# Attention and an MLP mixer on one core: the first normalization ahead of a branch, seven products of the identity, and one element's x through GpSimd

## The chip, the cores and the metric

The kernel runs on one core of a Trainium2 chip. Five engines work side by side, each through its own instruction queue: TensorE (PE; its weight loads are listed apart as PEld), VectorE (DVE), ScalarE (ACT), GpSimd (POOL) and SyncE (SP), which here issues nearly all DMAs. An engine works through its queue in order. Before an instruction starts, the semaphores that it waits for must have been raised by other engines or by landed DMAs. The metric is the device time of one execution in microseconds (us); lower is better.

## The reference, cut to what matters

```python
# q, k, v: (8, 12, 448, 64); all float32
def _attn_ref(q, k, v, g_q, g_k):
    def rmsnorm(x, g):
        rms = np.sqrt(np.mean(x * x, axis=-1, keepdims=True) + 1e-06)
        return x / rms * g
    q_n, k_n = (rmsnorm(q, g_q), rmsnorm(k, g_k))
    scale = 1.0 / np.sqrt(q.shape[-1])
    scores = scale * np.matmul(q_n, k_n.transpose(0, 1, 3, 2))
    scores = scores - np.max(scores, axis=-1, keepdims=True)
    attn = np.exp(scores)
    attn = attn / (np.sum(attn, axis=-1, keepdims=True) + 1e-09)
    return np.matmul(attn, v)

# heads are put side by side: x is (8, 448, 768)
def _moe_ref(x, w_tok1, w_tok2, w_ch1, w_ch2):
    h = np.maximum(x.transpose(0, 2, 1) @ w_tok1, 0.0) @ w_tok2
    u = x + h.transpose(0, 2, 1)
    h2 = np.maximum(u @ w_ch1, 0.0) @ w_ch2
    return u + h2
```

There are eight elements in the batch. For each, attention over twelve heads makes x; then a token MLP and a channel MLP run on x.

## The kernel before, in words

**Tiling.** Heads go in pairs, six pairs to an element and 48 in all; pair p lies with its two heads in the two halves of the partitions. For a pair, q and k are loaded, squared on ScalarE (`square`, L1435), summed on VectorE (`reduce`, L1451), turned into inverse roots by a guess and three Newton steps (`roots`: L1473, then L1492 to L1494 on VectorE, or L1481 to L1484 on GpSimd for later pairs), scaled (`scale`, L1502) and transposed (`turn_qk`, L430 on TensorE, copied out by ScalarE at L436 and L438). `score` (L456) multiplies k with q and ScalarE takes the exponential (L460); `values` (L529) multiplies with v; `ones` (L509) makes the row sums.

**The branch.** Softmax runs without subtracting the maximum unless the gains are large. `Start`, ahead of the branch, loads the first pairs, computes from the gains whether they are (`large`, L1340), and squares pairs 0 and 1. Every engine then loads the flag and jumps (L1539). All else is in `whole`, which is built twice, once for each arm; with this data the second arm runs. It begins with `first_pairs`: VectorE's reductions, roots and scalings of pairs 0 and 1. The loads that SP issues behind its own jump begin with v (L409), further q and k (L1412) and weights (L223). VectorE also has four passes over each loaded piece of weights (L346 to L351, then L380, with a pass on ScalarE at L357 between): the matrices come as 64-bit floats and are made into 32-bit ones.

**The MLP of an element.** The x of an element is turned and brought into the layout for the token MLP. For the first element TensorE does it. For the others VectorE transposes 32x32 blocks into `xt` (L827, `trans_x`), `send_x` writes them to DRAM in four DMAs of 32 rows each (`xs`, L789), and `load_x` reads them back in five (`x`, L798 and L801). An element has two halves of three pairs, and each half goes its own way through `xt`, `xs` and `x`. `tok1` multiplies (L840; L847 is the remainder of 64 tokens, where both halves' remainders come one after the other), `tok2` (L882) adds into `uT`. Then the first channel product `ch1` runs on seven Strassen products (L1002), on sums that VectorE (T1, T2) and GpSimd (T3, T4; L906, L907) form in `moving_sums`, and the second (`plain_2`, L1051, for the second element; `ch2`, L1068, on fifteen products, for the third and later) after it. The seven products are computed in the order of B11, B21, T2, T3, T1, B22, T4. Weights come as units of 384 KB from DRAM (`load_units`, L930) into eight buffers; up to seven are loaded ahead.

**Weight forms.** The fifteen products of `ch2` need sums of weight blocks. They are made once, while the second element's MLP runs, in eight groups (`form_items`): four DMAs from SP load a group (L305 to L307), GpSimd does 16 additions (L321) and three copies (L325) and sends the result to DRAM in two DMAs (L311, L312). A unit of the fifteen products may be loaded only when all eight groups are formed.

**Order.** No scheduler moves anything. Items are written out in lists with estimated costs, merged in proportion, and run in that order. `later(us, fn)` puts a step off by so many estimated microseconds: when the running sum of costs has passed its due time, it is emitted at that place in the queues. So the due times of forms, of `send_x` and of `load_x` decide the place of their instructions between all others, on SP and GpSimd too. A due time isn't a time on the chip.

For the third element's second half, `trans_x` names due times 0.0 for the send, 0.25 for the step and 6.0 for the load:

```python
start, step, load = {(1, 1): (2.0, 0.5, 9.0), (2, 1): (0.0, 0.25, 6.0)}.get((b, half), (2.0, 2.0, 12.0))
```

`first_pairs`, `Start`, `send_x`, `load_x` and `form_items` are what the change touches:

Of the kernel before, what the change touches and what calls it, by code (L numbers as in the profile page):

```python
# [13 lines left out]
ALU = mybir.AluOpType  # L14
# [69 lines left out]
def whole(ctx, tc, shifted, pre, q, k, v, g_q, g_k, moe_w_tok1, moe_w_tok2, moe_w_ch1, moe_w_ch2, out):  # L84


    nc = tc.nc
    ctx.enter_context(tc.manual_schedule(engines={
        e.engine for e in (nc.tensor, nc.vector, nc.scalar, nc.gpsimd)}))

    B, H, S, D = q.shape
    C = H * D
    DT = moe_w_tok1.shape[1]
    DC = moe_w_ch1.shape[1]
    P = 128
# [10 lines left out]
    KC, KF = NC // 2, NF // 2  # L106
    assert S % NS == 0 and R <= P and 2 * D == P and H % 2 == 0 and NC == NPAIR
    assert DT % P == 0 and C % P == 0 and DC % P == 0 and HC <= 512 and HC % P == 0 and S <= 512
# [5 lines left out]
    NM = S // P  # L114
# [27 lines left out]
    ident, one_c, expo_c, g_t = pre.ident, pre.one_c, pre.expo_c, pre.g_t  # L142
# [7 lines left out]
    ws2 = dram.tile([P, NF9 * 8, P], F32, name="ws2")  # L150

    st = dict(pre.st)
    pre.first_pairs(st)
    m_tile = lambda: ps_M.tile([P, 512], F32, name="m_ps", tag="M")
    s_tile = lambda name: ps_S.tile([P, 512], F32, name=name, tag="S")

    clock, pending = [0.0], []

# [133 lines left out]
    def form_items():  # L292


        G, FORMS_FROM, FORMS_EVERY = range(8), 55.0, 18.0
        plain = lambda g: wp2[:].rearrange("p (m h x k t) n -> p x h t m k n", m=3, h=2, x=2, k=3)[
            :, g // 4, g // 2 % 2, g % 2]
        made = ws2[:].rearrange("p (f c) n -> p c f n", c=8)
        eight = lambda t: t[:].rearrange("p n w -> p (n w)").bitcast(F32).rearrange("p (q n) -> p q n", q=8)

        def load(g):
            a, b, c = st["form", g] = [eight(raw_tile()) for _ in range(3)]
            src = plain(g)
            for m in range(2):
                nc.sync.dma_start(out=a[:, 3 * m:3 * m + 3], in_=src[:, m])  # L305
            nc.sync.dma_start(out=a[:, 6:8], in_=src[:, 2, 0:2])
            nc.sync.dma_start(out=b[:, 7], in_=src[:, 2, 2])  # L307

        def send(g):
            a, b, c = st.pop(("form", g))  # L310
            nc.gpsimd.dma_start(out=made[:, g, 0:8], in_=c)  # L311
            nc.gpsimd.dma_start(out=made[:, g, 8:NF9], in_=b[:, 0:7])  # L312
            st["formed"] += 1

        def part(g, i):
            a, b, c = st["form", g]
            at = dict(d=a[:, 4], s=a[:, 6], v=a[:, 7], y=a[:, 3])
            at.update({(m, k): a[:, 3 * m + k] if 3 * m + k < 8 else b[:, 7] for m in range(3) for k in range(3)})
            at.update({f: c[:, f] if f < 8 else b[:, f - 8] for f in range(NF9)})
            for o, x, op, y in W_STEPS[4 * i:4 * i + 4]:  # L320
                nc.gpsimd.tensor_tensor(  # L321
                    out=at[o], in0=at[x], in1=at[y], op=ALU.add if op == "+" else ALU.subtract)
            if i == 3:
                for f, x in W_SINGLE:
                    nc.gpsimd.tensor_copy(out=at[f], in_=at[x])  # L325
                send(g)

        for g in G:
            at = FORMS_FROM + g * FORMS_EVERY
            later(at, lambda g=g: load(g))  # L330
            for i in range(4):
                later(at + 8.0 + 2.5 * i, lambda g=g, i=i: part(g, i))
# [450 lines left out]
    def send_x(b, half, t, step):  # L783


        xs = st["xs", b, half] = xs_pool.tile([KC * S, P], F32, name="xs")

        def part(i):
            nc.sync.dma_start(  # L789
                out=xs[:, i:i + 32].rearrange("(n t) c -> t n c", t=32),  # L790
                in_=t[i:i + 32].rearrange("t (n c) -> t n c", c=32))
        for i in range(0, P, 32):
            later(i * step / 32, lambda i=i: part(i))

    def load_x(b, half):
        x, xs = x_tile(b, half), st.pop(("xs", b, half))[:].rearrange("(j s) n -> s j n", j=KC)
        for j in range(KC):
            nc.sync.dma_start(  # L798
                out=x[:, j, 0:NM, :], in_=xs[0:NM * P, j].rearrange("(c p) n -> p c n", p=P))
        for a in range(2):  # L800
            nc.sync.dma_start(out=x[a * D:(a + 1) * D, :, NM, :], in_=xs[NM * P:S])  # L801

    def x_tile(b, half):
        st["x", b, half] = x_pool.tile([P, KC, NS, P], F32, name="x", tag="x")
        return st["x", b, half]
# [496 lines left out]
class Start:  # L1302


    def __init__(self, ctx, tc, q, k, g_q, g_k, w2, g2, gate):
        self.nc = nc = tc.nc
        self.q, self.k = q, k
        B, H, S, D = q.shape
        self.NPAIR, self.NS, self.D = H // 2, 4, D
        self.R = S // self.NS  # L1310
        P = 128
        pool = lambda name, bufs: ctx.enter_context(tc.tile_pool(name=name, bufs=bufs))
        const = pool("start", 1)
        KF = w2.shape[0] // P // 2
        self.hb = const.tile([P, HB, 4, S // 2], F32, name="hb")

        flat = self.hb[:].rearrange("p q f s -> p (q f s)")
        n, o = 4 * self.NS * D, self.NPAIR * 4 * self.NS * D
        self.st = {("qk", p): flat[:, p * n:(p + 1) * n] for p in range(self.NPAIR)}
        self.qkT = [flat[:, o + i * 2 * S:o + (i + 1) * 2 * S].rearrange("p (i s) -> p i s", i=2) for i in range(3)]  # L1320
        assert flat.shape[-1] >= o + 3 * 2 * S
        self.v_0 = const.tile([P, S], F32, name="v_first")[:]
        self.first_slot = self.NPAIR
        self.far = 3 * self.NPAIR + 2
        qk_t = const.tile([P, 2, n], F32, name="qk_t")
        self.qk_t = [qk_t[:, i, :] for i in range(2)]
        self.v_t = [const.tile([P, S], F32, name=f"v_{i}")[:] for i in range(3)]

        warm = const.tile([P, 1], F32, name="warm")
        nc.vector.memset(warm[:], 1.0)  # L1330
        self.load_qk(0, self.st, other=nc.scalar)
        self.load_qk(1, self.st, other=nc.scalar)
        nc.scalar.activation(out=warm[:], in_=warm[:], func=AF.Square)
        gg = gate.tile([1, D], F32, name="gg")
        most = gate.tile([1, 1], F32, name="most")
        self.large = large = gate.tile([1, 1], I32, name="large")
        nc.vector.tensor_tensor(out=gg[:], in0=g2[:, 0, :], in1=g2[:, 1, :], op=ALU.mult)
        nc.vector.tensor_tensor(out=gg[:], in0=gg[:], in1=gg[:], op=ALU.mult)
        nc.vector.tensor_reduce(out=most[:], in_=gg[:], axis=AX_X, op=ALU.max)
        nc.vector.tensor_scalar(large[:], most[:], SCORE_BOUND**2 / D, None, ALU.is_gt)  # L1340
        self.g_t = const.tile([P, 2], F32, name="g_t")
        for i, g in enumerate((g_q, g_k)):
            for a in range(2):
                nc.gpsimd.dma_start(
                    out=self.g_t[a * D:(a + 1) * D, i:i + 1], in_=g.rearrange("(p o) -> p o", o=1))
        self.ident = const.tile([P, P], F32, name="ident")
        make_identity(nc, self.ident[:, :])
        self.one_c = const.tile([P, D], F32, name="one_c")
        nc.gpsimd.memset(self.one_c[:], 1.0)
        self.expo_c = const.tile([P, 1], F32, name="expo_c")  # L1350
        nc.gpsimd.memset(self.expo_c[:], -896.0 * 2**23)
        self.sq = const.tile([P, 4 * self.NS, D + 1], F32, name="sq")


        self.sq_2 = flat[:, 0:4 * self.NS * (D + 1)].rearrange("p (r d) -> p r d", d=D + 1)
        self.sq_1 = qk_t[:].rearrange("p i n -> p (i n)")[:, 0:4 * self.NS * (D + 1)].rearrange(
            "p (r d) -> p r d", d=D + 1)
        for sq in (self.sq, self.sq_1):
            self.summand(sq)
        for p in (2, 3):  # L1360
            for part in self.loads(p, self.st, nc.gpsimd, nc.gpsimd):
                part()
        self.rs_0 = const.tile([P, 8 * self.NS], F32, name="rs_0")
        for p in range(2):
            self.square(p, self.st)

    def first_pairs(self, st):

        D = self.D
        self.reduce(0, st)  # L1370
        self.reduce(1, st)
        for part in self.roots(0, st):
            part()
        self.scale(0, st)
        self.nc.vector.scalar_tensor_tensor(
            out=self.g_t[:, 0:1], in0=self.g_t[:, 0:1], scalar=float(D) ** 0.5, in1=self.g_t[:, 1:2],
            op0=ALU.mult, op1=ALU.mult)
        self.scale(1, st)

    def heads(self, p):  # L1380
        b, j = divmod(p, self.NPAIR)
# [192 lines left out]
```

## Time and profile before

| | |
|---|---|
| median of 3 runs | 1281.13 us (1280.30 to 1282.95) |
| the profiled execution | 1280.59 us |
| its span, first to last instruction | 1278.8 us |
| granted TensorE clock, mean | 0.997 |
| TensorE busy | 98% of the span |
| VectorE, ScalarE, GpSimd busy | 62%, 31%, 31% |
| DMA, mean | 179 GB/s |

Times within a trace are counted from the span's first instruction. An engine's share of busy time is an average over stages that have different limits; where an engine waits, the profile names what ended the wait. In a line of the timeline stand the start, the time taken, the engine, the line of the kernel, the operation, the tiles (out<-in), the shape and the number of instructions merged into the line; in brackets at the end stands how long the engine was idle before and what ended it. SPq and the like are an engine's queue: waits, jumps and the issuing of DMAs. A line of waits reads: engine, tile and line of what waited, what it waited for, us in total, how often, the longest. The answer for one line of the kernel gives, for each operation, the count, the duration in ns (min/median/max) and the first and last start.

### The profile page before, as it was taken

The page shows a single profiled execution, that of the slowest core. Times are in us where ns is not written, and L with a number is a line of the kernel's source. Part 1 is how long each engine was busy: PE and PEld are TensorE (multiplying, and loading weights), DVE is VectorE, ACT ScalarE, POOL GpSimd, SP SyncE. Part 2 cuts the span into 40 slices and gives each one's busy share as a digit, 9 for nine tenths or more (in the row PEclk, how much of TensorE's full clock was granted, in tenths as well). Part 3 has the DMA queues.
Part 4 walks back from the last instruction along what each step waited for, and adds up shares of the span by engine and source line. Part 5 has one row for each costly group of instructions (what it writes and reads, how often), then busy time and mean ns, then how long its engine had stood idle before and what let it go on. Part 6 is the DMA issues. An engine that isn't in the chain of part 4 may idle for free.

```text
span 1278.8 us, 20023 instructions
## 1 busy us (share of the span) xinstructions
PE 1249.1 (98%) x7236; PEld 887.4 (69%) x7236; DVE 796.8 (62%) x1241; ACT 393.6 (31%) x785; POOL 394.8 (31%) x637
## 2 busy tenths in 40 slices
PE   5999999999999899999999999999999999999998
PEld 2444444457745487796778768885887867797998
DVE  6999869756663355855668356765558456554233
ACT  6663433124330144402433044311343024300210
POOL 2302552043995611331223112241122322131222
PEclk9999999999999899999999999999999999999999
DMA  8767486999789876695657767585766865386554
GB/s 204 172 179 200 144 228 167 217 260 253 212 220 236 188 171 162 140 258 112 161 151 178 190 143 187 139 220 120 188 158 146 234 130 144 114 207 142 191 173 105
DMA packets 486784, 228.37 MB, mean 179 GB/s; under 512 B 368276, under 2 KB 446996, under 8 KB 486676
## 3 DMA queue, kind: packets, MB, share of 16 engines
q1 hardware_dynamic: 479682, 213.33, 67.5%
q0 software_dynamic: 3968, 12.98, 3.3%
q8 instruction: 59, 0.97, 0.3%
q10 hardware_dynamic: 3026, 0.69, 0.3%
q14 instruction: 49, 0.40, 0.1%
HBM read 184.26 MB, written 42.66 MB: 177 GB/s over the span
## 4 chain that ended last, share of the span: by engine, by line
PE 88%; DVE 5%; DMA 2%; SPq 1%; ACT 1%; issue 1%; DVEq 0%; ACTq 0%
PE m_ps L1002 25%; PE m_ps L1068 22%; PE s_ps L456 9%; PE o_ps L529 9%; PE m_ps L882 6%; PE m_ps L972 5%; PE m_ps L1051 4%; PE m_ps L840 2%; PE t_ps L840 2%; PE d_ps L509 1%; PE m_ps L509 1%; DVE es L497 1%; DVE raw L349 1%; DVE raw L347 1%; PE t_ps L430 1%
## 5 line engine op out<-in xcount | busy, mean ns | idle before, releaser
L1068 PE MATMUL m_ps<-hb,unit 128*128 128x224 f32 x1440 | 277.2, 354 | 0.0
L1068 PEld LDWEIGHTS m_ps<-hb,unit 128*128 128x128 f32 x1440 | 271.0, 190 | 8.9 <-issue 7.7
L1002 PE MATMUL m_ps<-tu,unit 128*128 128x224 f32 x1008 | 201.6, 355 | 1.3 <-ACT r L1012 1.3
L1002 PEld LDWEIGHTS m_ps<-tu,unit 128*128 128x128 f32 x1008 | 189.1, 190 | 15.0 <-issue 9.2
L460 ACT ACTIVATE e<-s_ps 128x448 f32<-128x448 f32 x294 | 138.7, 553 | 178.4 <-PE s_ps L456 169.8
L1002 PE MATMUL m_ps<-uT,unit 128*128 128x224 f32 x756 | 151.1, 354 | 0.0
L1002 PEld LDWEIGHTS m_ps<-uT,unit 128*128 128x128 f32 x756 | 142.2, 190 | 6.9 <-issue 3.9
L456 PE MATMUL s_ps<-qkT 64*64 64x448 f32 x1260 | 143.7, 545 | 0.8 <-ACT x L822 0.8
L529 PE MATMUL o_ps<-e,v 64*64 64x448 f32 x1148 | 129.4, 538 | 0.3 <-ACT uT L566 0.2
L497 DVE TENSOR_TENSOR es<-es,e 128x896 f32<-128x896 f32 x90 | 101.8, 1131 | 13.3 <-ACT e L460 8.6
L1008 DVE TENSOR_TENSOR hb<-m_ps,r 128x448 f32<-128x448 f32 x63 | 39.2, 622 | 108.8 <-POOL r L1008 56.7
L1008 POOL TENSOR_TENSOR hb<-r,r 128x448 f32<-128x448 f32 x21 | 23.8, 1132 | 246.0 <-ACT r L1024 246.0
L456 PEld LDWEIGHTS s_ps<-qkT 64*64 64x64 f32 x1260 | 44.9, 132 | 70.1 <-issue 60.6
L529 PEld LDWEIGHTS o_ps<-e,v 64*64 64x64 f32 x1148 | 45.1, 133 | 63.9 <-issue 60.4
L1481 POOL TENSOR_TENSOR nt<-rs 128x56 f32<-128x56 f32 (+1 forms) x54 | 22.4, 415 | 196.4 <-DVE rs L1473 193.6
L1009 ACT ACTIVATE hb<-hb 128x448 f32<-128x448 f32 x84 | 48.4, 577 | 99.4 <-DVE hb L1008 77.7
L321 POOL TENSOR_TENSOR raw<-raw 128x128 f32<-128x128 f32 x128 | 65.1, 528 | 34.6 <-DMA raw<-wp 30.1
L1083 POOL TENSOR_TENSOR uT<-uT,r 128x448 f32<-128x448 f32 x42 | 51.4, 1238 | 78.5 <-DVE r L1083 46.7
L882 PE MATMUL m_ps<-w_sb,h 128*128 128x448 f32 x192 | 75.2, 544 | 0.0
L1451 DVE TENSOR_REDUCE ms<-sq 128x28 f32<-128x896 f32 (+2 forms) x44 | 47.4, 1079 | 36.3 <-ACT sq L1438 28.2
L1008 DVE TENSOR_TENSOR r<-m_ps,r 128x448 f32<-128x448 f32 x42 | 26.1, 622 | 64.5 <-PE m_ps L1002 64.5
L887 DVE TENSOR_TENSOR uT<-uT,m_ps 128x448 f32<-128x448 f32 x48 | 29.4, 614 | 59.1 <-PE m_ps L882 59.0
(148 smaller groups left out, 1607.8 us busy)
## 6 DMA issues: line engine op xcount, KB each, us to landing
unit<-ws SPq DMA_DIRECT2D x267, 384.0 KB, 4.1
raw<-in_moe_w_ch_dram SPq DMA_DIRECT2D x72, 256.0 KB, 3.5
v<-in_v_dram SPq DMA_DIRECT2D x96, 112.0 KB, 4.1
out_dram<-turned SPq DMA_DIRECT2D x182, 56.0 KB, 1.9
xs<-xt SPq DMA_DIRECT2D x56, 168.0 KB, 4.6
qk_t<-in_q_dram SPq DMA_DIRECT2D x144, 56.0 KB, 3.6
qk_t<-in_k_dram SPq DMA_DIRECT2D x144, 56.0 KB, 3.7
x<-xs SPq DMA_DIRECT2D x42, 192.0 KB, 3.7
```

The lines of the kernel that those rows point to most:

```text
L321: nc.gpsimd.tensor_tensor(out=at[o], in0=at[x], in1=at[y], op=ALU.add if op == "+" else ALU.subtract)
L456: nc.tensor.matmul(out=pss[i][rows_of(i, a), 0:S], lhsT=qkT[h, 1, k * D:(k + 1) * D], rhs=qkT[h, 0, :], start=True, stop=True)
L460: nc.scalar.activation(out=e[:, i, :], in_=pss[i][:, 0:S], func=AF.Exp)
L497: nc.vector.tensor_tensor(out=es[:], in0=(es if k > 1 else st["e", t, 0])[:], in1=st["e", t, k][:], op=ALU.add)
L529: nc.tensor.matmul(out=st["o", p][a * D:(a + 1) * D, 0:S], lhsT=vt[rows, k * D:(k + 1) * D], rhs=e[rows, :], **kw)
L840: nc.tensor.matmul(out=st["t1", h][jc][:, 0:HC], lhsT=w1_sb[:, c, jc * P:(jc + 1) * P], rhs=st["x", b, h][:, :, c, :], start=start and c = ...
L882: nc.tensor.matmul(out=ps[:, 0:S], lhsT=st["h1", jc][:, cc * P:(cc + 1) * P], rhs=w2_sb[:, jc].rearrange("p c r -> p (c r)"), start=(jc == ...
L972: nc.tensor.matmul(out=ps, lhsT=a[:, o + 2 * half, :], rhs=natural(half * KF + t) if wide else u[:, half * KC + t, :], start=(t == 0 and h ...
L1002: nc.tensor.matmul(out=ps[:, j * HS:(j + 1) * HS], lhsT=w[:, t, j, :], rhs=m, start=(t == 0), stop=(t == KC - 1))
L1008: add = lambda e, o, x, y: e.tensor_tensor(out=o, in0=x, in1=y, op=ALU.add)
L1068: nc.tensor.matmul(out=ps[:, x * HS:(x + 1) * HS], lhsT=st["w"][:, tile_at % 6, :], rhs=hb[:, X_SLOT[f], i, :], start=(i == 0), stop=(i == 3))
L1083: e.tensor_tensor(out=get(out), in0=get(x_), in1=get(y), op=ALU.add if op == "+" else ALU.subtract)
```

## The change

- VectorE's first chain (`first_pairs`) is moved from the head of `whole` into `Start`. It now stands ahead of the branch, once instead of once in each arm. Its small tiles come from a pool of their own (`st_0`).
- In its place TensorE multiplies the identity with itself seven times, into a bank of the scores' pool that nobody reads.
- For the third element's second half (element 2, half 1), the four DMAs of `send_x` and the five of `load_x` are issued by GpSimd instead of SP.
- Groups 6 and 7 of the forms are due 26 estimated us later.

```diff
     st = dict(pre.st)
-    pre.first_pairs(st)
...
+    first_ps = s_tile("first_ps")
+    for _ in range(7):
+        nc.tensor.matmul(out=first_ps[:, 0:P], lhsT=ident[:, :], rhs=ident[:, :], start=True, stop=True)
...
-        G, FORMS_FROM, FORMS_EVERY = range(8), 55.0, 18.0
+        G, FORMS_FROM, FORMS_EVERY, FORMS_REST = range(8), 55.0, 18.0, 26.0
...
-            at = FORMS_FROM + g * FORMS_EVERY
+            at = FORMS_FROM + g * FORMS_EVERY + (FORMS_REST if g > 5 else 0.0)
             later(at, lambda g=g: load(g))
...
         def part(i):
-            nc.sync.dma_start(
+            x_queue(b, half).dma_start(
                 out=xs[:, i:i + 32].rearrange("(n t) c -> t n c", t=32),
                 in_=t[i:i + 32].rearrange("t (n c) -> t n c", c=32))
...
+    def x_queue(b, half):
+        return nc.gpsimd if (b, half) == (2, 1) else nc.sync
+
     def load_x(b, half):
+        e = x_queue(b, half)
         x, xs = x_tile(b, half), st.pop(("xs", b, half))[:].rearrange("(j s) n -> s j n", j=KC)
         for j in range(KC):
-            nc.sync.dma_start(
+            e.dma_start(
                 out=x[:, j, 0:NM, :], in_=xs[0:NM * P, j].rearrange("(c p) n -> p c n", p=P))
         for a in range(2):
-            nc.sync.dma_start(out=x[a * D:(a + 1) * D, :, NM, :], in_=xs[NM * P:S])
+            e.dma_start(out=x[a * D:(a + 1) * D, :, NM, :], in_=xs[NM * P:S])
...
-        for p in range(2):
-            self.square(p, self.st)
-
-    def first_pairs(self, st):
-
-        D = self.D
-        self.reduce(0, st)
-        self.reduce(1, st)
-        for part in self.roots(0, st):
-            part()
-        self.scale(0, st)
-        self.nc.vector.scalar_tensor_tensor(
-            out=self.g_t[:, 0:1], in0=self.g_t[:, 0:1], scalar=float(D) ** 0.5, in1=self.g_t[:, 1:2],
-            op0=ALU.mult, op1=ALU.mult)
-        self.scale(1, st)
+        with tc.tile_pool(name="st_0", bufs=1) as self.st_pool:
+            self.nt_pool = self.st_pool
+            for p in range(2):
+                self.square(p, self.st)
+            self.reduce(0, self.st)
+            self.reduce(1, self.st)
+            for part in self.roots(0, self.st):
+                part()
+            self.scale(0, self.st)
+            nc.vector.scalar_tensor_tensor(
+                out=self.g_t[:, 0:1], in0=self.g_t[:, 0:1], scalar=float(D) ** 0.5, in1=self.g_t[:, 1:2],
+                op0=ALU.mult, op1=ALU.mult)
+            self.scale(1, self.st)
```

What the queues of the arm that runs hold then, compared with before: TensorE's has the seven products ahead of its first transposes, and nothing else differs. VectorE's has the flag's load and the jump behind the second scaling instead of ahead of the first reduction. ScalarE's is the same. On GpSimd, group 5 is followed by the twelve Newton steps of a later pair, then the nine DMAs of x, then group 6, then group 7 with the moving sums T3 and T4 of the third element between its parts. On SP the nine DMAs of x are gone, the loads of group 6 stand behind the first three units of the third element and the loads of group 7 behind six output DMAs; a few loads of v, of q and of units change places with each other further on.

## The prediction

> **What bounds the kernel now.** I read the page's busy line first, then TensorE's waits, then a table by stage around the largest of them, and last the timelines of the engines that feed it.
>
> ```profile
> PE 1249.1 (98%) x7236; PEld 887.4 (69%) x7236; DVE 796.8 (62%) x1241; ACT 393.6 (31%) x785; POOL 394.8 (31%) x637
> ...
> PE t_ps L430 <- DVE hb L1502: 14.4, 1, 14.4
> PE t_ps L847 <- DMA x<-xs: 5.2, 1, 5.2
> ```
>
> TensorE is busy for 1249.1 of 1278.8 us. Two holes make 19.6 of the other 29.7 us: 14.4 us before its first transpose, and 5.2 us at 421.8, where the third element's second half of x isn't there. No other wait exceeds 1.3 us. The change works on these two.
>
> The table by stage (us, busy us of PE, PEld, DVE, ACT, POOL, granted clock, DMA share, GB/s) and TensorE's timeline show that the second hole costs more than its length; the last three lines are the same place one element later, without a wait.
>
> ```profile
> 422.00:427.00 5.00, 0.00 (x0) 0.00 (x0) 0.00 (x0) 0.74 (x2) 4.69 (x12) 0.72 1.07 342
> 427.00:430.00 3.00, 2.93 (x6) 1.58 (x7) 0.22 (x1) 0.00 (x0) 2.42 (x8) 0.50 1.10 187
> ...
> 420.92 0.92 PE L847 MATMUL m_ps<-x,w_sb 64*128 64x384 f32 x4
> 427.07 2.07 PE L847 MATMUL t_ps<-x,w_sb 64*128 64x384 f32 x4 [5.24 <-DMA x<-xs]
> 433.99 9.28 PE L882 MATMUL m_ps<-w_sb,h 128*128 128x448 f32 x24
> ...
> 576.40 0.92 PE L847 MATMUL m_ps<-x,w_sb 64*128 64x384 f32 x4
> 577.15 0.81 PE L847 MATMUL t_ps<-x,w_sb 64*128 64x384 f32 x4
> 581.87 9.29 PE L882 MATMUL m_ps<-w_sb,h 128*128 128x448 f32 x24
> ```
>
> The clock is down to 0.50 when work comes back. From L847 to L882 it is 433.99 - 420.92 = 13.07 us here and 581.87 - 576.40 = 5.47 us there: the hole is worth 7.60 us, 5.24 of waiting and 2.36 at half clock.
>
> Why x is late, by the timelines of SP and GpSimd:
>
> ```profile
> 409.62 0.32 SPq L789 DMA_DIRECT2D xs<-xt  x1
> 410.27 2.54 SPq L930 DMA_DIRECT2D unit<-ws  x1
> 412.87 3.45 SPq L789 DMA_DIRECT2D xs<-xt  x3
> 419.05 1.44 SPq L798 DMA_DIRECT2D x<-xs  x3
> 420.52 2.47 SPq L801 DMA_DIRECT2D x<-xs  x2
> ...
> 406.82 3.81 POOL L321 TENSOR_TENSOR raw<-raw 128x128 f32<-128x128 f32 x8 [13.86 <-DMA raw<-wp]
> ```
>
> The data (xt) is complete at 404.21 (L827: 403.59 + 0.62), but SP sends it from 409.62 to 416.32, behind forms' loads, v and units, with the DMA engines at a share of about 1. GpSimd sits idle for 13.86 us meanwhile.
>
> The branch, by the answer for its line:
>
> ```profile
> L1539 PEldq COMPARE_BRANCH  x1: 5444/5444/5444, 3.7 to 3.7; - x1
> L1539 DVEq COMPARE_BRANCH  x1: 67/67/67, 3.7 to 3.7; - x1
> L1539 ACTq COMPARE_BRANCH  x1: 45/45/45, 8.8 to 8.8; - x1
> ...
> 8.76 1.30 DVE L1451 TENSOR_REDUCE ms<-sq 112x8 f32<-112x520 f32 x2 [5.73 <-ACT qk_t L1435]
> ```
>
> VectorE branches at 3.75 and starts its first reduction at 8.76: 5.0 us. The squares it needs ended at 6.41, so ScalarE, which the line names, didn't hold it; the jump did. ScalarE's own jump ends at 8.85 and its next instruction starts at 12.60, at most 3.75 us.
>
> [...]
>
> **The change part by part.**
>
> *VectorE's first chain ahead of the branch.* It has 19 instructions, from 8.76 to 16.11. Its last input is the second half of pair 1's squares, at 9.14 (ScalarE, already ahead of the branch). Reductions of pair 0 fit in the idle time after 6.41; the last of pair 1 then runs about 9.2 to 9.9, so the roots start at 9.95 instead of 11.30: 1.35 us earlier. The transposes can start at 13.1, not 14.45. In exchange VectorE jumps later. Its sequencer ran ahead: the last DVEq wait of L1502 is at 14.0, the instruction starts at 15.43. Less 1.35, the load of the flag comes at 12.65, 0.54 + 0.07 later (durations from L1539) the jump, 13.3. [...]VectorE returns at 17.0 to 18.3; its next reduction started at 16.03.
>
> What that does is read from VectorE's and ScalarE's timelines:
>
> ```profile
> 27.22 0.43 DVE L346 TENSOR_SCALAR cv_sb<-raw 128x512 uint32<-128x512 uint32 x1 [0.79 <-DMA raw<-in_moe_w_tok_dram]
> ...
> 47.66 0.78 ACT L357 ACTIVATE raw<-raw,expo_c 128x512 uint32<-128x512 uint32 x1 [0.97 <-DVE raw L351]
> ```
>
> From 27.22 to 78 VectorE never idles, and 27.22 is set by a DMA that SP issues, which the change leaves alone. At 47.66 ScalarE waits for VectorE; the exponentials behind it free the bank that TensorE's transposes at 48.91 need. So TensorE's time at 48.9 hangs on VectorE's at 27.22. Gained microseconds before it become waits there: worth 0. Lost ones count: between 16.03 and 27.22 VectorE waits 0.57 + 0.79 = 1.36 us that a delay can use up, so a return after 17.39 costs the difference, 0 to 0.9 us. I take 0.3, nearer ScalarE's jump[...]. Bounds for the whole head: -1.5 (the 48.9 link is looser than I read it) to +1.0.
>
> *Seven products of the identity.* A 128x384 product of L840 takes two records, 12 records in 3.87 us; so 128 columns take 0.645 / 3 = 0.215 us at full and 0.43 at half clock: 7 x 0.43 = 3.0 us. They run at 9.1 to 12.1, after TensorE's jump and before the transposes at 13.1: cost 0, with 1.0 us of cover. If they wake the clock, the 16 transposes (3.22 us in front, 1.75 at 28.84) finish sooner, which is again lost at 48.9.
>
> *x sent by GpSimd, forms 6 and 7 later.* On GpSimd the order becomes form 5, the twelve root steps, 4 + 5 DMAs of x, form 6, form 7 with the moving sums T3 and T4 between its parts. The roots' input is there at 402.08 (L1473) and took 4.26 us (L1481 to L1484, 410.59 to 414.85): the first send goes at 406.4. Price of a send: GpSimd's DMAs took 0.52 us with 64 pieces and 0.77 with 512, so 0.00055 us for each further piece; a send of 32x42 = 1344 pieces of 128 bytes is estimated at 1.2 us. Nearest row from below: 0.77; above, no row reaches so far. Four end at 411.3; GpSimd's DMAs landed 3.2 to 6.3 us after issue; with 4, the last at 410.1 lands at 414.1. The five loads cost 3 x 0.70 + 2 x 0.60 = 3.3 us, the last starts at 416.8, and with 3.7 to 4 lands at 420.7. TensorE wants it at 421.8: the wait goes, and the clock stays up. Gain 7.6.
>
> What is late next: SP loses 9 DMAs of x and form 6's 4 loads ahead of its units, so units and output come earlier. GpSimd ends its x loads at 417.4; form 6 (16 sums 7.47 at 421.22, three copies 0.76, two sends 0.90 + 0.98) ends at 427.6, half of form 7 at 431.4, and with the three pairs of sums (1.5 each), the other half and its sends the last T3 is ready near 444. TensorE wants T3 after 12 records of T2, 454.02 + 2.3 - 7.6 = 448.7: hidden, 4 us to spare. The finished forms are read from 514.9 on.
>
> *Sum:* 1280.59 (profiled run) - 7.6 + 0.3 = 1273.3. The median of the runs shown is 0.54 above that run, so 1273.8; I say 1273.7.
>
> **The rivals.**
>
> - *x comes later than TensorE wants it.* SP's backlog shares the DMA engines (share about 1), so both of x's legs stretch. Landing at 424.5 instead of 420.7 leaves 2.7 us of waiting and about 1 us of slow clock: 1277.5. Against: the sends now start 3.2 us earlier, finish 5 us earlier, and 640 KB of form loads are behind them.
> - *The head's gain survives.* Chain 1.35 us earlier and warm transposes: up to 2 us. For it: 14.4 us is the largest wait. Against: the 0.97 us wait for VectorE. About 1271.8.
> - *Slower:[...]* Its queue is in order: sends, loads, forms and T3 stand in one line. If a send costs 2.7 us rather than 1.2, the four take 6 us more, x lands at 426.7 and nothing is gained; from there each further 0.25 us a send costs 1 us. At 3.5 us x lands at 430, and T3 slips with it: 1284.
> - *No gain.* x is in time, but the 7.6 us return as a wait for SP's output sends (24 of 0.85 us, from about 412 on) or for GpSimd's sums: 1280.
>
> **How the numbers follow.** My case 0.60, x later 0.20, head's gain 0.10, no gain 0.05, slower 0.05. 0.2% is 2.6 us, about what a measurement can tell. Faster by more: 0.60 + 0.10 + 0.19 = 0.89; same 0.06; slower 0.05. The range 1271.3 to 1278.3 takes in the head's bounds and most of the late cases; about 0.15 is left out.
>
> **What would show it.** Right: no wait of L847 for x, clock 1.00 from 410 to 440, L882 near 426.4; sends of about 1.2 us on POOL from 406; first transposes near 13.1 but transposes of L430 still near 48.9; VectorE back at 17 to 18.3. Wrong: sends over 2.5 us, L1002 waiting for tu from POOL, VectorE back after 19, or TensorE ahead of the old trace at 60.

## The result, and the profile after

The changed kernel takes 1274.9 us (median of four executions, 1273.18 to 1277.11), the kernel before 1281.35 beside it: ratio 0.9953, 95% interval 0.9934 to 0.9971. On another chip it was 1275.94 against 1280.99, ratio 0.9958 (0.9944 to 0.9972). The forecast was 1273.7. The profiled execution is the slowest of the four, 1277.11 us with a span of 1275.3.

Line numbers of the changed kernel are higher by 3 from the forms on, and by 5 or 7 further down: L840, L847 and L882 of before are L847, L854 and L889. TensorE's waits (engine, tile, line, who ended the wait; us in total, times, longest):

```profile
PE first_ps L158 <- DVE ms L1456: 9.1, 1, 9.1
PE t_ps L433 <- ACT e L463: 2.2, 3, 1.0
...
PE t_ps L854 <- DMA x<-xs: 1.3, 1, 1.3
```

TensorE now starts at 9.14 instead of 14.45. In its place there is a new wait, three times for ScalarE's exponentials, 2.2 us. The wait for x has shrunk from 5.2 to 1.3 us. x's place in the timelines of TensorE and GpSimd (start, us, engine, line, operation; in brackets the idle time before it):

```profile
422.86 0.92 PE L854 MATMUL m_ps<-x,w_sb 64*128 64x384 f32 x4
425.06 1.37 PE L854 MATMUL t_ps<-x,w_sb 64*128 64x384 f32 x4 [1.28 <-DMA x<-xs]
426.36 4.14 PE L847 MATMUL t_ps<-x,w_sb 128*128 128x384 f32 x12
430.34 9.36 PE L889 MATMUL m_ps<-w_sb,h 128*128 128x448 f32 x24
...
407.38 3.51 POOL L792 DMA_DIRECT2D xs<-xt  x4
417.88 2.29 POOL L805 DMA_DIRECT2D x<-xs  x3 [6.99 <-PE m_ps L1058]
420.16 1.26 POOL L808 DMA_DIRECT2D x<-xs  x2
```

From L854 to L889 it is 430.34 - 422.86 = 7.48 us, where before had 13.07 and an undisturbed place 5.47: of the hole's 7.60 us, 5.59 are gone. A send costs GpSimd 3.51 / 4 = 0.88 us. After the fourth, GpSimd waits 6.99 us until all of them have landed, and only then issues the loads. (The bracket names TensorE's L1058, but the fourth send, issued at 410.02, took 7.2 us to land, until 417.2; in three other traces the same line names that DMA.)

The head, by the timelines of VectorE and ScalarE:

```profile
17.46 1.24 DVE L1456 TENSOR_REDUCE ms<-sq 112x16 f32<-112x1040 f32 x1 [2.86 <-ACT e L463]
27.58 0.43 DVE L349 TENSOR_SCALAR cv_sb<-raw 128x512 uint32<-128x512 uint32 x1 [0.84 <-DMA raw<-in_moe_w_tok_dram]
...
48.00 0.76 ACT L360 ACTIVATE raw<-raw,expo_c 128x512 uint32<-128x512 uint32 x1 [1.46 <-DVE raw L354]
```

VectorE is back from its jump at 17.46. At 27.58 it waits for the same load from SP as before, which landed 0.36 us later, and ScalarE's use of the result follows at 48.00, after 47.66 before. In between, ScalarE's wait grew from 0.97 to 1.46 us. So in this execution the lead of the head goes where the forecast sent it.

How far TensorE is ahead can be followed matmul by matmul (start of the same matmul in this trace less its start in the trace of before, by its time before): -1.67 us at 14.45, -0.79 at 28.84, +0.32 at 48.91, +1.94 at 330, then -3.65 at 434 and to the end. The hole at x gives 5.6 us, and 1.6 us are lost between 49 and 330, where the change touches nothing.

### The profile page after: what moved, and what is told of

It is laid out like the page before. It is cut to its first block, busy times and chain, and to the rows that moved or that the text cites. A ratio compares the mean times of both kernels' runs of the same rounds, so it can differ in the third digit from the quotient of the medians.

```text
span 1275.3 us, 20054 instructions
## 1 busy us (share of the span) xinstructions
PE 1250.6 (98%) x7250; PEld 888.1 (70%) x7250; DVE 797.2 (63%) x1241; ACT 393.1 (31%) x785; POOL 401.2 (31%) x646
## 4 chain that ended last, share of the span: by engine, by line
PE 88%; DVE 6%; SPq 1%; DMA 1%; ACT 1%; issue 1%; POOL 0%; DVEq 0%; ACTq 0%; POOLq 0%
PE m_ps L1009 26%; PE m_ps L1075 22%; PE s_ps L459 9%; PE o_ps L532 9%; PE m_ps L889 6%; PE m_ps L979 5%; PE m_ps L1058 4%; PE m_ps L847 2%; PE t_ps L847 2%; PE d_ps L512 1%; DVE raw L350 1%; DVE raw L352 1%; PE m_ps L512 1%; DVE es L500 1%; PE t_ps L433 1%
## 5 line engine op out<-in xcount | busy, mean ns | idle before, releaser
L1009 PE MATMUL m_ps<-tu,unit 128*128 128x224 f32 x1008 | 201.6, 355 | 1.3 <-ACT r L1019 1.3
L1009 PEld LDWEIGHTS m_ps<-tu,unit 128*128 128x128 f32 x1008 | 189.1, 190 | 15.0 <-issue 9.2
L1009 PE MATMUL m_ps<-uT,unit 128*128 128x224 f32 x756 | 151.2, 354 | 0.7 <-DVE hb L1015 0.7
L1009 PEld LDWEIGHTS m_ps<-uT,unit 128*128 128x128 f32 x756 | 142.2, 190 | 7.7 <-issue 4.6
L500 DVE TENSOR_TENSOR es<-es,e 128x896 f32<-128x896 f32 x90 | 102.4, 1138 | 13.4 <-ACT e L463 8.8
L889 PE MATMUL m_ps<-w_sb,h 128*128 128x448 f32 x192 | 75.3, 544 | 0.3 <-DVE uT L894 0.3
L324 POOL TENSOR_TENSOR raw<-raw 128x128 f32<-128x128 f32 x128 | 68.0, 551 | 21.7 <-DMA raw<-wp 17.2
```

The lines of the kernel that those rows point to most:

```text
L324: nc.gpsimd.tensor_tensor(out=at[o], in0=at[x], in1=at[y], op=ALU.add if op == "+" else ALU.subtract)
L500: nc.vector.tensor_tensor(out=es[:], in0=(es if k > 1 else st["e", t, 0])[:], in1=st["e", t, k][:], op=ALU.add)
L889: nc.tensor.matmul(out=ps[:, 0:S], lhsT=st["h1", jc][:, cc * P:(cc + 1) * P], rhs=w2_sb[:, jc].rearrange("p c r -> p (c r)"), start=(jc == ...
L1009: nc.tensor.matmul(out=ps[:, j * HS:(j + 1) * HS], lhsT=w[:, t, j, :], rhs=m, start=(t == 0), stop=(t == KC - 1))
```

## The experiments

Four kernels first took the change apart: the x part alone, the head alone, and the x part's two halves, each on top of the head.

**The x part alone** (head as before, no products; the edit is against the changed kernel, and what is left of it is the same as before with the x part put in):

```
+    pre.first_pairs(st)
-    first_ps = s_tile("first_ps")
...
-        with tc.tile_pool(name="st_0", bufs=1) as self.st_pool:
...
+    def first_pairs(self, st):
```

> Only the x part: x's sends and loads of the third element's second half on GpSimd and forms 6 and 7 later; VectorE's chain stays behind the branch and there are no products of the identity. Theory (the whole gain is x's hole, the head is worth nothing): as fast as the changed kernel, -5.5 to -7 us against before (ratio 0.9946 to 0.9957); from L847 to L882 (both shifted by 3 lines here) about 7.5 us instead of 13.07; the first transposes at 14.4 as before. Rival (the head's gain survives, and the last microsecond of the changed kernel's gain comes from it): -4 to -5 us. Rival (DMA engines, not the queue, hold x): the last DMA of x again lands 1 to 2 us after TensorE wants it, as in the changed kernel, whose profile had 1.28 us of it.

**The head alone:**

```
-        G, FORMS_FROM, FORMS_EVERY, FORMS_REST = range(8), 55.0, 18.0, 26.0
+        G, FORMS_FROM, FORMS_EVERY, FORMS_REST = range(8), 55.0, 18.0, 0.0
...
-        return nc.gpsimd if (b, half) == (2, 1) else nc.sync
+        return nc.sync
```

> Only the head: VectorE's first chain ahead of the branch and the seven products; x stays on SP, forms 6 and 7 at their old places. Theory (TensorE's time at 48.9 hangs on VectorE's at 27.2, and that on a DMA from SP): within 0.6 us of before, ratio 0.9995 to 1.0005, TensorE 1.5 to 2.5 us ahead of before's trace up to 28 us and not ahead at all after 49. Rival (the head's gain survives): -1.5 to -2.4 us, ratio 0.9981 to 0.9988, TensorE still ahead at 60 us. Rival (VectorE comes back late from its jump): +0.6 to +1 us.

**GpSimd's queue without the later forms** (the first of the two edits above):

> The changed kernel with forms 6 and 7 at their old places. GpSimd's order is then half of form 6, the roots, the other half, its two sends, the four sends of x, a quarter of form 7, the five loads of x, the rest of form 7. Theory (a queue that passes SP helps only if GpSimd's own queue is clear): the roots end at 414.8 as before, form 6 at 421.2, so x's sends end at 424.8 and x lands at 434 to 437 instead of 427; hole 7 to 10 us longer than before's: 1288 to 1292 us, ratio 1.005 to 1.008. Rival (the forms' delay is a trifle, the other queue does it): as the changed kernel, 1275 us.

**Later forms without GpSimd's queue** (the second):

> The changed kernel with x's sends and loads on SP and forms 6 and 7 later. SP then has eight loads of forms fewer ahead of x's first send, but three of the sends still stand behind a unit's load that waits for its buffer, and a form's four loads stand between the sends and x's loads. Theory (the queue is what holds x): x lands about as late as before, 425 to 429; 1278 to 1282 us, ratio 0.998 to 1.0005. Rival (the forms' loads and their DMA traffic are what held x): x on time, 1274 to 1276 us, ratio 0.994 to 0.996.

What was measured, these and all later runs; each of the three blocks ran on a chip of its own, beside the kernel before. The fifth column counts executions whose mean granted clock is listed as 0.998 or less. Four profiled executions are listed so, and each has a slow stretch on the way: the first trace of before (0.997) a clock of 0.50 from 424.18 to 431.00, which takes 0.5 x 6.82 / 1278.8 = 0.0027 off its mean; the x part alone (0.998) 0.50 at 426.70 to 429.80; early weights with FORMS_REST 40 (0.998) 0.50 at 312.80 to 316.00; the queue only (0.992) 12 matmuls of L847 in 5.99 us instead of 4.14. So I take the column as an estimate of how often an execution had such a stretch; one at 0.999 can still hide a shorter one.

```
kernel                          median us  ratio to before (95%)      range us           at 0.998 or less
x part alone                    1278.89    0.9992 (0.9981 to 1.0004)  1275.8 to 1283.2   12 of 22
head alone                      1275.89    0.9972 (0.9960 to 0.9984)  1274.1 to 1283.3    6 of 22
head, queue only                1293.65    1.0097 (1.0076 to 1.0118)  1292.1 to 1297.8    6 of  6
head, later forms only          1275.24    0.9962 (0.9947 to 0.9978)  1273.6 to 1276.0    0 of  9
  before, beside these          1279.88                               1275.4 to 1284.3   29 of 46
changed kernel again            1275.94    0.9958 (0.9944 to 0.9972)  1273.7 to 1276.8    0 of  5
FORMS_REST 56                   1277.70    0.9975 (0.9962 to 0.9989)  1275.5 to 1283.1    1 of  9
FORMS_REST 56, x on SP          1277.29    0.9972 (0.9959 to 0.9986)  1276.0 to 1279.4    0 of  9
no products of the identity     1277.51    0.9973 (0.9964 to 0.9982)  1273.7 to 1281.3    7 of 22
  before, beside these          1280.99                               1276.4 to 1284.3   26 of 33
before again                    1280.70    1.0002 (0.9988 to 1.0015)  1275.1 to 1285.4    8 of 14
old head, FORMS_REST 40         1278.11    0.9983 (0.9969 to 0.9997)  1275.7 to 1283.0    3 of 14
changed, early weights          1276.49    0.9970 (0.9957 to 0.9983)  1275.1 to 1281.4    4 of 14
early weights, FORMS_REST 40    1275.30    0.9958 (0.9946 to 0.9970)  1272.5 to 1282.6    5 of 22
  before, beside these          1280.81                               1276.7 to 1284.7   37 of 51
```

The first two contradict the forecast's sum. The x part alone, taken at 7.6 us, brings 1.0 (0.5 slower to 2.4 faster by the interval); the head alone, taken at a loss of 0.3, brings 3.6 (2.0 to 5.1). In its profile the x part alone has 1.65 us of waiting and a half-clock stretch left (0.50 at 426.70 to 429.80), 9.48 us from L851 to L886 (one rival had said so: x again 1 to 2 us late), and 12 of its 22 executions are at 0.998 or less. So on the old head the x part doesn't even clear the hole each time.

The head alone has no listed wait for x in its profile, with x on SP as before (5.99 us from L854 to L889, against 5.47 undisturbed); TensorE is ahead by 1.69 us at 14.45 and by 0.76 at 48.91, so neither the "not at all" of my theory nor the 1.5 to 2.4 of its rival. The list of executions says where to look: the kernel before spreads over 9 us, 1275.4 to 1284.3, and its fastest are as fast as the changed kernel.

The two halves of the x part are plain. With GpSimd's queue and forms where they were, the kernel is 13.8 us slower than before, and 17.8 slower than the head alone. GpSimd's and TensorE's timelines of that run:

```profile
423.43 3.48 POOL L792 DMA_DIRECT2D xs<-xt  x4
...
436.49 2.31 POOL L805 DMA_DIRECT2D x<-xs  x3 [7.75 <-DMA xs<-xt]
...
443.31 1.81 PE L854 MATMUL t_ps<-x,w_sb 64*128 64x384 f32 x4 [15.91 <-DMA x<-xs]
```

x stands behind form 6 in GpSimd's own line, its first send goes 16 us later than in the changed kernel, and TensorE waits 15.91 us. The place is as expected, the time 1.7 us above the range given.

With later forms alone, x on SP, I expected next to nothing and the rival was right: 1275.24 us, and not one of nine executions at 0.998 or less. That is as fast as the changed kernel. Against the head alone, on the same chip, it is 0.65 us by the medians, and the intervals overlap: what the later forms add to the head isn't settled. SP's and TensorE's timelines:

```profile
400.44 0.32 SPq L792 DMA_DIRECT2D xs<-xt  x1
401.01 1.07 SPq L937 DMA_DIRECT2D unit<-ws  x1
402.13 5.47 SPq L792 DMA_DIRECT2D xs<-xt  x3
...
411.03 1.44 SPq L805 DMA_DIRECT2D x<-xs  x3
412.51 1.24 SPq L808 DMA_DIRECT2D x<-xs  x2
...
419.91 0.92 PE L854 MATMUL m_ps<-x,w_sb 64*128 64x384 f32 x4
420.66 0.81 PE L854 MATMUL t_ps<-x,w_sb 64*128 64x384 f32 x4
```

xt was complete at 399.68 (VectorE's last transpose), so SP sent it 0.8 us later; before, it was 5.4 us later (404.21 to 409.62), with a form's four loads in between. SP's last load of x is issued at 413.75, and TensorE finds x there at 420.66. From the first send to the last load's issue SP needs 413.75 - 400.44 = 13.3 us here and 13.4 before; GpSimd needs 421.42 - 407.38 = 14.0 in the changed kernel. GpSimd's queue is no faster; once forms 6 and 7 were moved it had no forms ahead of x's first send, and SP's hadn't either.

**The kernel before once more,** unchanged:

> The kernel before once more, for a second trace of it and as a null comparison. If its hole at x is the same in every execution: 5.2 us of waiting for x and 13 us from L847 to L882 again. Second theory (the hole comes and goes with the DMA backlog): another length, anywhere from 0 to 7 us of waiting, and SP's sends of x at another distance from TensorE; times spread over 8 us, their granted clock between 0.996 and 1.000. Ratio 1.000 within 0.15% either way.

Its second trace is the key to the rest. TensorE's timeline:

```profile
420.97 0.92 PE L847 MATMUL m_ps<-x,w_sb 64*128 64x384 f32 x4
423.10 1.39 PE L847 MATMUL t_ps<-x,w_sb 64*128 64x384 f32 x4 [1.21 <-DMA x<-xs]
424.42 4.14 PE L840 MATMUL t_ps<-x,w_sb 128*128 128x384 f32 x12
428.39 9.29 PE L882 MATMUL m_ps<-w_sb,h 128*128 128x448 f32 x24
```

The same program, and the hole is 1.21 us of waiting without a slow stretch: 7.42 us from L847 to L882 instead of 13.07. This execution took 1275.07 us. Why x is earlier shows on ScalarE and VectorE. First the lines of the trace that the forecast was made from, then the same lines of the second:

```profile
398.49 0.95 ACT L1438 ACTIVATE sq<-qk_t 128x896 f32<-128x896 f32 x1 [15.08 <-DMA qk_t<-in_k_dram]
...
399.47 1.08 DVE L1451 TENSOR_REDUCE ms<-sq 128x28 f32<-128x896 f32 x1 [8.75 <-ACT sq L1438]
...
403.59 0.62 DVE L827 STREAM_TRANSPOSE xt<-uT 128x448 f32<-128x448 f32 x1
```

```profile
393.29 0.95 ACT L1438 ACTIVATE sq<-qk_t 128x896 f32<-128x896 f32 x1 [10.54 <-DMA qk_t<-in_k_dram]
...
394.27 1.09 DVE L1451 TENSOR_REDUCE ms<-sq 128x28 f32<-128x896 f32 x1 [3.50 <-ACT sq L1438]
...
399.71 0.64 DVE L827 STREAM_TRANSPOSE xt<-uT 128x448 f32<-128x448 f32 x1
```

The transposes that make xt stand in VectorE's queue behind a reduction; the reduction waits for ScalarE's squares, and these for a pair of q and k that SP loads between 374 and 396, with the DMA engines at a share of 0.89. The squares start 5.2 us earlier the second time, the reduction with them, and xt is complete 3.9 us earlier. SP sends it 5.0 us later (405.38), as it did before (5.4 us), so the gain goes through to x, although TensorE stood at the same place (0.06 us apart at 417). In these two traces, then, x's hole is set by how far SP and its loads have got, and 7.60 us was one draw. With x on GpSimd the sends hang on the same loads, through the roots that GpSimd works off ahead of them: in seven traces it waits 6.5 to 9.3 us for VectorE before it can begin these.

**The changed kernel again, and three variants.** The variants change one number (26.0 to 56.0, with x on GpSimd and on SP), or leave out the seven products.

> The changed kernel once more, beside the three below. First theory (all the gain is x's hole of 7.6 us, the head is worth nothing): ratio 0.9945 to 0.9955 whatever the chip, and the x part alone should have shown it, which it didn't (0.9992). Second theory, formed on the first four runs (the hole at x comes and goes between executions of the kernel before, about 0 to 7.6 us with the backlog of the DMA engines; the head keeps about 2.5 us on average; x on GpSimd itself lands 1.3 to 1.7 us too late): 1275 to 1277 us, ratio 0.9965 to 0.998, that is no better than the head alone (0.9972).

> The changed kernel with FORMS_REST 56 instead of 26: forms 6 and 7, their eight loads on SP among them, come after x, T3 and T4. Second theory (what makes x late on GpSimd is the traffic that shares the DMA engines): 1 MB less beside x, which takes some 4 us at 250 GB/s, so x lands 2 to 4 us earlier and the wait of 1.3 to 1.7 us goes: 1 to 2 us below the changed kernel. Rival (GpSimd's way of sending is slow by itself): x's wait stays at 1.3 us or more, as the changed kernel within 0.5 us.

> As the run with FORMS_REST 56, but x on SP: VectorE's chain and the products first, forms after T4, no other queue. Second theory (the forms' loads ahead of x and their traffic were the backlog; with them gone SP's queue is good enough): as fast as the run on GpSimd or faster, 1273 to 1275 us, ratio 0.994 to 0.9965, no run with a granted clock below 0.999. Rival (x needs a queue of its own): 2 us or more slower than with x on GpSimd.

> The changed kernel without the seven products of the identity. If the products matter by the clock: the transposes and first scores of the head run at half clock until 16 to 20 us, 1 to 2 us later than with them, and as ScalarE's first exponentials come later, 0.5 to 1.7 us of it stays to the end: ratio to the changed kernel 1.0004 to 1.0013. If TensorE's time at 48.9 hangs on VectorE's first conversion at 27.2 in every execution: no difference (within 0.3 us).

The changed kernel came out better than the second theory said, below the head alone, though the intervals overlap (0.9944 to 0.9972, 0.9960 to 0.9984). In its second trace TensorE waits 0.28 us for x. With FORMS_REST 56 the wait for x is gone on both queues. On GpSimd the sends land after a median of 6.5 us, against 6.9 and 7.1 in the two traces of the changed kernel, so the removed megabyte hardly shortened them. (The 250 GB/s of the expectations is near what the traces moved from 400 to 430: 258 in the first of before, 248 in the changed kernel, 209 with the megabyte gone.) The loads behind them land in 3.4 and 3.0 us (those of 192 and of 96 KB), against 4.7 and 4.7, and 4.5 and 6.8: the reason given fits them, by one trace.

The times that I expected, 1 to 2 us below the changed kernel and 1273 to 1275 us on SP, did not come: 1277.70 and 1277.29. In both traces form 7's results are written at 463 to 466 instead of 445, and a v is late; that the first causes the second is not shown. TensorE's waits in these two runs, GpSimd first:

```profile
PE o_ps L532 <- DMA v<-in_v_dram: 1.1, 1, 1.1
```

```profile
PE o_ps L532 <- DMA v<-in_v_dram: 1.8, 2, 1.3
```

Around it TensorE loses 2.9 and 3.6 us between 470 and 500 (against the trace of before); the two traces of the changed kernel lose nothing there.

Without the products the median is 1.6 us above the changed kernel's, with overlapping intervals. Its trace has the transposes at 3.22 us, as before, instead of 2.49, and TensorE 1.25 us ahead at 48.91, as far as the best trace with products (1.14). Neither the one trace nor the overlapping intervals can price the products.

**Two more sizes.** The old head with FORMS_REST 40 and x on GpSimd; the changed kernel with one exchange on SP; and the exchange together with FORMS_REST 40:

```
-        if i < 2:
-            load_v(2 + i)
+        if i == 1:
+            load_v(2)
+            load_v(3)
```

> The x part alone on the head of before, with FORMS_REST 40 instead of 26: form 6's four loads go behind the six units on SP. It takes the traffic of 0.5 MB away from in front of x's sends, 2 us at 250 GB/s. If that clears x (no wait over 0.5 us, no execution with a granted clock below 0.998), the difference to before is the mean price of before's hole. First theory: 7.6 us, ratio 0.994. Second theory: 3 to 4 us, ratio 0.997 to 0.9977.

> The changed kernel with one exchange on SP: the second chunk of the token weights is loaded ahead of the v of pair 2 instead of behind it, 2 to 3 us earlier. If TensorE's time at 48.9 hangs on VectorE's conversion at 27.2 through 20.4 us of work, and that on this load: VectorE's first conversion of that chunk has no DMA wait and starts at 26.0 to 26.7 instead of 27.6, ScalarE's use of it at 46.5 to 47.1, and TensorE at 49 is 1.0 to 1.9 us ahead of before's trace instead of 0.3 behind; 0 to 1 us off the mean time of the changed kernel (0.9955 to 0.9960 against before). Rival (that load isn't the pin): ScalarE's use stays at 47.7 to 48 and TensorE with it.

> Both together, the early weights and FORMS_REST 40: x without a wait over 0.5 us, the head 1 to 1.9 us ahead at 49, and no wait for v near 480 of the kind that FORMS_REST 56 brought (1.1 and 1.8 us), because form 7's results are written some 10 us earlier: 1273 to 1275 us, ratio 0.9945 to 0.9955, the best of all. Rival: the traffic that is moved comes back as another wait behind 430, then as the changed kernel or worse (0.9958 to 0.997).

The first is the nearest to a price for x by itself: ratio 0.9983 (0.9969 to 0.9997), 2.2 us, with 3 of 14 executions still at 0.998 or less. In its trace TensorE waits 0.95 us at that place; the bracket names ScalarE, but x's first 96 KB load, issued at 421.88, took 3.7 us, until 0.1 us before TensorE went on at 425.68. So x isn't cleared, as the expectation required, and 2.2 us is not the whole price of the hole. It is less than the 3 to 4 us of the second theory, and far from 7.6. The executions of before on that chip say much the same: the 37 of 51 at 0.998 or less take 3.4 us longer on average than the others (1281.64 and 1278.19), which is 2.5 us in the mean, wherever on the way their stretches lie.

The early weights do at 49 us what was expected. VectorE's and ScalarE's timelines:

```profile
26.53 0.42 DVE L349 TENSOR_SCALAR cv_sb<-raw 128x512 uint32<-128x512 uint32 x1
...
46.92 0.78 ACT L360 ACTIVATE raw<-raw,expo_c 128x512 uint32<-128x512 uint32 x1 [0.97 <-DVE raw L354]
```

No wait for the load, 26.53 and 46.92, and TensorE is 0.73 us ahead at 48.91, a little under the range given. The distance from the one line to the other is 20.39 us; it lies between 20.38 and 20.60 in all nine other traces with the new head too. So the link that the forecast named is real. But the time didn't gain (0.9970). The load isn't always late: in six traces with the old order of loads VectorE doesn't wait for it.

The combination ran into something else. TensorE's timeline of that run:

```profile
308.78 0.92 PE L532 MATMUL o_ps<-e,v 64*64 64x448 f32 x4
311.18 1.41 PE L532 MATMUL o_ps<-e,v 64*64 64x448 f32 x4 [1.48 <-DMA v<-in_v_dram]
312.52 5.74 PE L1009 MATMUL m_ps<-tu,unit 128*128 128x224 f32 x20
```

A v comes late at 309, long ahead of the forms and x that were moved, and a half-clock stretch follows (0.50 at 312.80 to 316.00; L1009's 20 matmuls take 5.74 us): 4.6 us. The run with the queue only lost 4.8 us at the same place. There the wait is put down to VectorE, but in these two traces SP issues the first of that v's loads at 306.26 and 307.35, and by 304.52 in all others, so SP's backlog is the likelier cause in both. So there is a second hole that comes and goes. It costs 1.8 us in a third trace, on SP with FORMS_REST 56; all three have the new head, and three of ten are too few to say that it has to do with it.

At x the trace of the combination has no wait. Its head isn't 1 to 1.9 us ahead at 49, as expected, but 0.18: VectorE was back from its jump at 17.89 only, and began the conversion at 27.10 without waiting for the load. The median is 1275.3, ratio 0.9958 like the changed kernel's; nothing tried is better than that by more than its interval.

## Why the forecast was right, and where it wasn't

**The total** was right: 1274.9 and 1275.94 lie in the range, 1.2 and 2.2 us above the forecast. Its sum was not. The forecast took x's part 5 to 6 us too large and the head's 4 us too small; that these errors nearly cancel is luck.

**The step that failed is "the hole is worth 7.60 us".** Its length was read properly, from one execution. A second execution of the kernel before had 1.95 us of it (7.42 less 5.47). Measured over many executions, x's part on the old head is worth 1.0 us (0.5 slower to 2.4 faster), with FORMS_REST 40 it is 2.2 (0.4 to 4.0), not 7.6. The step behind it, "the wait goes, and the clock stays up", failed in part too: 1.28 us of waiting were left in the changed kernel's first profile, 1.65 us and a half-clock stretch in the x part alone. The sign of it was in front of me: three executions, 1280.30 to 1282.95, say nothing on how long one hole is in each.

**The head is worth more than nothing.** The mechanism (48.9 hangs on 27.2 through VectorE) holds in the traces, and in the profiled execution of after the gain was lost as said, +0.32 us at 48.91 where +0.3 was forecast. What I missed is that both ends move. VectorE starts its conversion anywhere from 25.99 to 27.58, later when SP's load is late. And in the old head TensorE itself is often the later of the two, by the pace of its first matmuls: the 22 scores of L456 behind the transposes take 3.4, 3.4, 4.2 and 4.2 us in four traces, and TensorE stands at -0.41, 0, +0.55 and +1.20 us at 48.91.

The table by stage shows the pace by the number of matmuls; its clock column lists 1.00 in both, so a late clock behind it is my estimate (us, busy us and number on PE, PEld, DVE, ACT, POOL, clock, DMA share, GB/s). Before, then the x part alone:

```profile
17.40:20.20 2.80, 2.73 (x22) 0.93 (x20) 2.18 (x6) 2.28 (x5) 0.00 (x0) 1.00 1.01 272
```

```profile
17.40:20.20 2.80, 2.80 (x13) 1.24 (x16) 2.28 (x7) 1.78 (x4) 0.00 (x0) 1.00 1.19 275
```

22 matmuls against 13 in the same 2.80 us. With the new head the 22 scores take 0.97 + 2.21 = 3.2 us in six traces, 1.01 + 2.21 without the products, and TensorE stands at -1.25 to +0.32. The means at 48.91 are +0.34 (four traces, old head) and -0.58 (seven, new head with products and old order of loads): about 0.9 us. That explains a part of the head's 3.6 us.

Another part goes with fewer executions at 0.998 or less (6 of 22 against 29 of 46), and why an earlier head should make slow stretches rarer 350 us later no trace shows. But these aren't all of the rest: among the executions at 0.999 or above alone, the head takes 1275.5 us on average and the kernel before 1277.9 (16 and 17 executions), 2.4 us apart where the traces show 0.9. So what the head gains beyond 0.9 us stays open; it may be partly chance, since the interval begins at 2.0 us. The parts measured one by one make 1.0 + 3.6 = 4.6 us by their ratios, the whole 6.0 and 5.4.

**Sends by GpSimd:** 0.88 us each where 1.2 was estimated. **Landing:** 6.9 us where 4 was taken from GpSimd's other DMAs; the loads' start at 417.88 instead of 414.1 comes from this, and the wait of 1.28 us is the rival "x comes later", in part. xs from SP landed in 4.1 to 6.4 us (medians of five traces). Form 6's loads, 640 KB in that rival, are 576 KB (two of 192, one of 128, one of 64).

**What needn't have been credited to the queue:** the forecast counted on GpSimd's queue to pass SP's line. With the head and the later forms but x on SP the kernel is as fast (0.9962), and the queue without later forms makes it 13.8 us slower than before. From the first send to the last load's issue it is 14.0 us on GpSimd and 13.3 on SP.

**Right as forecast:** VectorE back from its jump at 17.46, 4.2 us after it branches (17.0 to 18.3 said, which is 13.3 and the 3.75 to 5.0 us of the two jumps before; 16.72 to 17.89 in the traces with the new head; what sets the length of a jump was not shown, and the 0.3 us taken for it was an estimate); the guess of the roots at 9.50 and the transposes at 12.78 (9.95 and 13.1 said); the products 3.33 us at no cost (3.0 said); T3 hidden, its third part ready at 447.96 (444 said); clock 1.00 at x in the changed kernel's first trace (425.10 to 430.00), L847's 12 matmuls behind the wait in 4.14 us in both, and no mean below 0.999 in its nine executions.

## What to carry to other kernels

A hole in one profile is one draw: the one at x was 7.60 us in one trace of before and 1.95 in the other. Where it ends on a transfer while the DMA engines are full (a share of 1.07 here), take a second profile of the same kernel, and look at the spread of its times and granted clocks, before its length goes into a sum. Look upstream of a late transfer for what its data waits for: here a reduction ahead of the transposes in VectorE's queue, where squares 5.2 us earlier made xt 3.9 us earlier. And clear the queue you have before using a second one; the second has a line of its own (x behind form 6 on GpSimd: 15.91 us of waiting).

## What the runs showed of the hardware

- TensorE's first matmuls are slow, and for how long differs: the first 16 transposes take 3.22 us in the four traces with the old head, where the same 16 of the next pair take 1.75; the 22 scores behind the first take 3.4 us in two of these traces and 4.2 in the others. Behind the seven products (3.32 to 3.33 us) the first transposes take 2.49 to 3.10 us in six traces, without the products 3.22.
- A wait can cost more than it lasts. In the x part alone 1.65 us at x were followed by a clock of 0.50 (426.70 to 429.80), and 12 matmuls of L844 took 5.74 us instead of 4.14; in early weights with FORMS_REST 40, 1.48 us for a v were followed by 0.50 at 312.80 to 316.00. After 1.28 us in the changed kernel and 1.21 us in the second trace of before the clock was 1.00 (425.10 to 430.00, 423.10 to 428.00). In the first trace of before it fell while TensorE was still waiting: 1.00 until 424.18, 2.35 us into the 5.24, then 0.50 until 431.00. What decides whether it falls, and for how long, the traces don't settle.

  The two lines are the table by stage of the x part alone, the wait and what follows it:

```profile
423.00:426.00 3.00, 1.35 (x7) 0.58 (x6) 0.00 (x0) 0.87 (x2) 2.84 (x7) 1.00 0.99 178
426.70:429.80 3.10, 3.10 (x6) 1.76 (x6) 0.00 (x0) 0.00 (x0) 2.96 (x8) 0.50 0.35 54
```

- A DMA of 168 KB in pieces of 128 bytes took GpSimd 0.88 us to issue in eight traces (3.48 to 3.52 us for four).
